# Exponentials on VectorE as four shifted piecewise linear terms, added by the value matmuls, with two PSUM banks for them and projections in 32-column pieces

## The chip, the cores and the metric

One core of one Trainium2 chip runs the program. The metric is the device time in microseconds (us) of one execution, as the median over the runs of a kernel. ACT is ScalarE, DVE is VectorE, PE is TensorE, POOL is GpSimd. The profile of a kernel is one more execution, taken with the hardware profiler; "the records" are that execution's instruction records, and times in them are counted from the first record.

## The reference

Four blocks follow each other: multi-query attention (A), linear attention (B), A, B, each with a layer norm ahead and a residual around it. S = 2048 tokens, D = 512, H = 32 heads of 16.

```python
def _A_ref(x, wq, wk, wv, wo):              # one K and V head for 32 query heads
    q = (x @ wq).reshape(B, S, H, Dh).transpose(0, 2, 1, 3)
    k, v = x @ wk, x @ wv
    p = softmax(einsum("bhqd,bkd->bhqk", q, k) * Dh ** -0.5)
    return merge(einsum("bhqk,bkd->bhqd", p, v)) @ wo
def _B_ref(x, wqkv, wo):
    phi = lambda t: where(t > 0, t + 1, exp(t)) + 1e-6
    pq, pk = phi(q), phi(k)
    kv, z = einsum("bhsd,bhse->bhde", pk, v), einsum("bhsd->bhd", pk)
    return merge(einsum("bhqd,bhde->bhqe", pq, kv) / (einsum("bhqd,bhd->bhq", pq, z) + 1e-6)) @ wo
x = x + _A_ref(_layernorm(x), ...);  x = x + _B_ref(_layernorm(x), ...)     # twice
```

Block A needs 2 x 32 x 2048 x 2048 exponentials, which is 2 x 2048 = 4096 tiles of 128 x 512.

## The kernel before

A scheduler, written in Python and run while the program is built, simulates the engines with planned durations and fixes the order of the instructions on each engine. On the chip each engine follows its fixed list and waits on semaphores. A lower `prio` goes first.

```python
# a score set: 32-row matmuls into 2 or 3 PSUM banks, one exponential on ScalarE, then value matmuls from PTA
o = add(PE, ..., prio=0.0, name="sA", pk=("S", ...))
oe = add(AC, tac(m * 512), lambda e: e.activation(PTA[:, hp.idx, 0:m * 512], bank(3 * s, m * 512), ACTF.Exp, scale=SCALE), ...)
...
# some tiles go to VectorE: scores in bank 6, six operations per pair of tiles
o = add(DV, tdv(512), lambda e: e.tensor_scalar(out=xT[...], in0=bank(6), scalar1=SCALE * LOG2E * 65536.0, scalar2=127.0 * 65536.0, ...))
... # dpass: xu, xsq, xw, xl, xc (fp16 polynomial), xo (scalar_tensor_tensor into PTD as uint16, read as bf16)
...
# a "unit" of 64 tiles fills the one value accumulator (bank 7); norm() then hands it on
oe = add((DV, AC), ..., lambda e: copy(Eo[:, he.idx, :], bank(7)), acq=[he], rel=[h7], prio=0.0, name="evA")      # 2 Eo buffers
o = add(PE, 0.48, tr, ..., acq=[ht, hos] if par == 0 else [ht], rel=[he], prio=1.2, name="trA")                   # one bank, one of 2 Osb
...
def epi_tr(L, qb, g, hos, fine):
    pr = 4.0
    o = add(PE, 0.22, tr, ..., acq=[h], uses=[hos], rel=[hos], prio=pr, name="otr")                               # one bank; gives Osb back
...
def phi(h, o, dst, keys, prio, tiled=False):          # keeps the bank of the projection until its last step
    o1 = add(AC, tac(512), lambda e: e.activation(e_buf[:, he.idx, :], bank(h.idx), ACTF.Exp), ..., name="phe")
    o2 = add(DV, tdv(512, 0.52), lambda e: e.tensor_scalar(out=e_buf[...], in0=e_buf[...], scalar1=1.0, scalar2=1e-6, op0=ALU.min, op1=ALU.add), ..., name="phm")
    add(DV, tdv(512), lambda e: e.scalar_tensor_tensor(out=dst, in0=bank(h.idx), scalar=0.0, in1=e_buf[...], op0=ALU.max, op1=ALU.add), rel=[h, he], ...)
...
# b_prep, pr = 3.5: the query projections of block B
o = proj(h, [(wqkv_sb[...], xnT[...]) for ft in range(FT)], 512, ..., pr + 0.2, name="pq")
...
# Banks.take for such single banks: 6, or else 5 while it is lent
elif f[6]: got = 6
elif f[5] and self.share(): got = 5
```

The softmax here doesn't subtract the row's maximum and nothing guards it: scores larger than these inputs give would overflow.

## Time and profile before

| | before |
|---|---|
| median of the first 3 runs | 1764.62 us (1764.61 to 1767.42) |
| PE, DVE, ACT, POOL busy | 92, 91, 97, 2 % |
| chain that ended last | ACT 89 %, DVE 5 %, PE 5 % |
| exponential tiles on VectorE | 512 of 4096 |
| time at half TensorE clock | 3.4 us, in the tail |

The lines themselves stand in the prediction. In a line of groups come the source line, engine and operation, the tiles written and read, their shapes, the number of instructions, the busy time, the mean of one in ns, and then the idle time of the engine just before them with what ended it. ACT is on 89 % of the chain and almost always busy, so the time is ACT's work in the attention stretches plus a rest.

For all kernels below I split the records of the profiled run in the same way, so that the parts sum to the span: the exponentials of the attention at their unhindered spacing from start to start (1.330 us after one 1536 wide, 0.904 us after one 1024 wide, 0.478 us after one 512 wide), ACT's other work between the first and last exponential of a layer, ACT's time lost between them (apart for full and half TensorE clock), and the rest: ramp, layer change and tail. Before: 1592.5 + 49 + 21.8 + 0 + 99.7 = 1763 us.

### The profile page before, as it was taken

The page shows a single profiled execution, that of the slowest core. Times are in us where ns is not written, and L with a number is a line of the kernel's source. Part 1 is how long each engine was busy: PE and PEld are TensorE (multiplying, and loading weights), DVE is VectorE, ACT ScalarE, POOL GpSimd, SP SyncE. Part 2 cuts the span into 40 slices and gives each one's busy share as a digit, 9 for nine tenths or more (in the row PEclk, how much of TensorE's full clock was granted, in tenths as well). Part 3 has the DMA queues.
Part 4 walks back from the last instruction along what each step waited for, and adds up shares of the span by engine and source line. Part 5 has one row for each costly group of instructions (what it writes and reads, how often), then busy time and mean ns, then how long its engine had stood idle before and what let it go on. Part 6 is the DMA issues. An engine that isn't in the chain of part 4 may idle for free.

```text
span 1762.9 us, 27663 instructions
## 1 busy us (share of the span) xinstructions
PE 1621.9 (92%) x11447; PEld 511.0 (29%) x11533; DVE 1601.6 (91%) x2902; ACT 1714.9 (97%) x1553; POOL 28.0 (2%) x46
## 2 busy tenths in 40 slices
PE   7999999999998899999799999999989999999998
PEld 4222222222232223223342222222223222232224
DVE  7999988999889998899589998899999999989985
ACT  7999999999999999999699999999999999999995
POOL 0000000000000000000000000000000000000000
PEclk9999999999999999999999999999999999999999
DMA  3000000000000000000000000000000000000001
GB/s 121 1 1 1 1 1 1 1 1 1 1 1 1 1 1 1 1 1 1 1 1 1 1 1 1 1 1 1 1 1 1 1 1 1 1 1 1 1 1 48
DMA packets 7725, 9.14 MB, mean 5 GB/s; under 512 B 1456, under 2 KB 7088, under 8 KB 7600
## 3 DMA queue, kind: packets, MB, share of 16 engines
q1 hardware_dynamic: 7600, 7.37, 1.3%
q8 instruction: 90, 1.47, 0.3%
q14 instruction: 35, 0.29, 0.1%
HBM read 5.28 MB, written 2.10 MB: 4 GB/s over the span
## 4 chain that ended last, share of the span: by engine, by line
ACT 89%; DVE 5%; PE 5%; DMA 0%; issue 0%; SPq 0%
ACT PTA L809 86%; ACT e_buf L991 2%; PE ps_all L522 1%; PE ps_all L1112 1%; PE ps_all L661 1%; DVE stats L487 1%; PE ps_all L698 1%; DVE PTD L885 1%; DVE xn_buf L498 0%; DVE Kr L537 0%; DVE xT L863 0%; DMA x_sb<-in_A_x_dram 0%; DVE xnT L511 0%; PE ps_all L1110 0%; DVE pqT L1106 0%
## 5 line engine op out<-in xcount | busy, mean ns | idle before, releaser
L809 ACT ACTIVATE PTA<-ps_all 128x1536 bf16<-128x1536 f32 (+1 forms) x1307 | 1630.7, 1520 | 2.3 <-PE ps_all L661 1.4
L661 PE MATMUL ps_all<-QT,Kr 32*128 32x512 bf16 x4226 | 652.5, 384 | 84.3 <-ACT PTA L809 66.4
L698 PE MATMUL ps_all<-PTA,Vaug 128*32 128x512 bf16 x3584 | 548.7, 389 | 15.7 <-ACT PTA L809 11.0
L863 DVE TENSOR_SCALAR xT<-ps_all 128x512 int32<-128x512 f32 x512 | 349.7, 683 | 28.4 <-PE ps_all L661 25.6
L661 PEld LDWEIGHTS ps_all<-QT,Kr 32*128 32x128 bf16 x4226 | 159.9, 91 | 578.1 <-ACT PTA L809 404.1
L885 DVE SCALAR_TENSOR_TENSOR PTD<-xT,xs 128x1024 uint16<-128x1024 int32 x256 | 310.4, 1214 | 0.6
L947 PE MATMUL ps_all<-maskx,zer 128*32 128x512 bf16 x911 | 296.2, 381 | 0.3 <-DVE Eo L710 0.3
L698 PEld LDWEIGHTS ps_all<-PTA,Vaug 128*32 128x32 bf16 x3584 | 134.6, 93 | 359.9 <-issue 253.2
L880 DVE TENSOR_SCALAR xu<-xT 128x1024 f16<-128x1024 uint16 x256 | 174.6, 682 | 1.2
L884 DVE TENSOR_TENSOR xs<-xs,xu 128x1024 f16<-128x1024 f16 x256 | 174.0, 681 | 1.2
L881 DVE TENSOR_TENSOR xs<-xu 128x1024 f16<-128x1024 f16 x256 | 174.1, 680 | 1.0
L698 PE MATMUL ps_all<-PTD,Vaug 128*32 128x512 bf16 x512 | 137.0, 387 | 3.5 <-DVE PTD L885 1.8
L882 DVE TENSOR_SCALAR xs<-xs 128x1024 f16<-128x1024 f16 x256 | 106.3, 415 | 0.8
L883 DVE TENSOR_SCALAR xu<-xu 128x1024 f16<-128x1024 f16 x256 | 106.5, 416 | 0.0
L947 PEld LDWEIGHTS ps_all<-maskx,zer 128*32 128x32 bf16 x911 | 80.1, 95 | 72.4 <-issue 41.5
L522 PE MATMUL ps_all<-wqkv_sb,xnT 128*128 128x512 bf16 x230 | 67.6, 390 | 4.8 <-issue 3.3
L992 DVE TENSOR_SCALAR e_buf<-e_buf 128x512 f32<-128x512 f32 x64 | 27.0, 421 | 33.7 <-ACT e_buf L991 33.6
L991 ACT ACTIVATE e_buf<-ps_all 128x512 f32<-128x512 f32 x64 | 44.9, 712 | 6.3 <-PE ps_all L522 4.3
L495 POOL TENSOR_TENSOR rstd<-veps,mhalf 128x1 f32<-128x1 f32 x30 | 24.5, 818 | 1657.0 <-DVE veps L493 1657.0
L487 DVE BATCH_NORM_STATS2 stats<-x_sb 128x6 f32<-128x512 bf16 x64 | 43.2, 682 | 3.5 <-DMA x_sb<-in_A_x_dram 2.8
L698 PEld LDWEIGHTS ps_all<-PTD,Vaug 128*32 128x32 bf16 x512 | 30.7, 93 | 54.3 <-DVE PTD L885 23.8
L719 PE MATMUL ps_all<-identf,Eo 128*128 128x128 f32 x256 | 42.0, 286 | 2.5 <-ACT Eo L710 1.4
(89 smaller groups left out, 842.3 us busy)
## 6 DMA issues: line engine op xcount, KB each, us to landing
out_dram<-x_sb SPq DMA_DIRECT2D x16, 128.0 KB, 1.7
x_sb<-in_A_x_dram SPq DMA_DIRECT2D x3, 512.0 KB, 6.8
wqkv_sb<-in_B_wqkv_dram SPq DMA_DIRECT2D x1, 1536.0 KB, 11.3
x_sb<-in_A_x_dram SPq DMA_DIRECT2D x2, 256.0 KB, 3.5
wq_sb<-in_A_wq_dram SPq DMA_DIRECT2D x1, 512.0 KB, 4.7
wo_sb<-in_A_wo_dram SPq DMA_DIRECT2D x1, 512.0 KB, 7.9
wo_sb<-in_B_wo_dram SPq DMA_DIRECT2D x1, 512.0 KB, 11.1
wk_sb<-in_A_wk_dram SPq DMA_DIRECT2D x1, 16.0 KB, 2.5
```

What stands on the lines that cost most here:

```text
L522: i = e.matmul(bank(h.idx, n), lhsT=l, rhs=r, start=(c + k == 0), stop=(c + k == len(mms) - 1))
L661: x = e.matmul(bank(b0 + k), lhsT=Kr[r, m, kt * P:(kt + 1) * P], rhs=QT[r, self.units[u][0] % 2, gs, q0:q0 + n], start=True, stop=True)
L698: return e.matmul(ps[32 * c:32 * c + 32, 7 * 512:8 * 512], lhsT=Vaug[:, kt, :], rhs=src, start=opened[0], stop=opened[1], skip_group_check ...
L809: oe = add(AC, tac(m * 512), lambda e: e.activation(PTA[:, hp.idx, 0:m * 512], bank(3 * s, m * 512), ACTF.Exp, scale=SCALE), deps=[o] + pr ...
L863: o = add(DV, tdv(512), lambda e: e.tensor_scalar(out=xT[:, hx.idx, i * 512:(i + 1) * 512], in0=bank(6), scalar1=SCALE * LOG2E * 65536.0, ...
L880: o = add(DV, tdv(w, 0.52), lambda e: e.tensor_scalar(out=u_, in0=lo, scalar1=1.0 / 65536, scalar2=-0.5, op0=ALU.mult, op1=ALU.add), deps= ...
L881: o1 = add(DV, tdv(w, 0.52), lambda e: e.tensor_tensor(out=s_, in0=u_, in1=u_, op=ALU.mult), deps=[o] + c["prev"], name="xsq", **kw)
L882: o2 = add(DV, tdv(w, 0.26), lambda e: e.tensor_scalar(out=s_, in0=s_, scalar1=XK, scalar2=-XW, op0=ALU.mult, op1=ALU.add), deps=[o1], nam ...
L883: o3 = add(DV, tdv(w, 0.26), lambda e: e.tensor_scalar(out=u_, in0=u_, scalar1=1.0, scalar2=XL, op0=ALU.mult, op1=ALU.add), deps=[o1], nam ...
L884: o4 = add(DV, tdv(w, 0.52), lambda e: e.tensor_tensor(out=s_, in0=s_, in1=u_, op=ALU.mult), deps=[o2, o3], name="xc", **kw)
L885: o5 = add(DV, tdv(w), lambda e: e.scalar_tensor_tensor(out=PTD[:, hp.idx, 0:w].bitcast(U16), in0=xT[:, k, 0:w], scalar=2.0 ** -9, in1=s_, ...
L947: f = lambda e: e.matmul(ps[32 * c:32 * c + 32, 7 * 512:8 * 512], lhsT=zer[:, 0:32], rhs=maskx[:].bitcast(BF16)[:, 0:512], start=not owned ...
```

## The change

It lets VectorE compute far more exponentials with less work each. It adds a bias to the scaled score and writes it as uint16, whose bits read as bf16 are a piecewise linear 2^x. Three copies with 32, 64 and 96 added shift the breaks. The value matmuls add the four terms, with weights folded into four scaled copies of V. VectorE gets two PSUM banks, ScalarE fixed sets of three and two. Projections are cut into four matmuls of 32 columns, so they run in the tiling mode of the value matmuls.

```diff
-            if len(c["pos"]) == 2:
+            if len(c["p1"]) == 4:
...
-            o = add(DV, tdv(w, 0.52), ... name="xu");  o1 ... "xsq";  o2 ... "xw";  o3 ... "xl";  o4 ... "xc"
-            o5 = add(DV, tdv(w), lambda e: e.scalar_tensor_tensor(out=PTD[:, hp.idx, 0:w].bitcast(U16), ...), name="xo")
+            for r in range(NTERM):
+                dep = c["p1"]
+                if r:
+                    dep = [add(DV, tdv(512 * m, 0.26), lambda e, r=r: e.tensor_scalar(out=PTD[:, hp.idx, r, 0:512 * m],
+                               in0=PTD[:, hp.idx, 0, 0:512 * m], scalar1=float(SHIFT[r]), scalar2=None, op0=ALU.add), ..., prio=3.0, name="xo")]
+                for i, p in enumerate(c["pos"]):
+                    pv = self.add_pv(p, PTD[:, hp.idx, r, i * 512:(i + 1) * 512].bitcast(BF16), hp, dep[0 if r else i], r, 1)
...
-    NPA, NPD, NDX = 5, 6, 3
+    NPA, NPD = 5, 3
...
+    DB = (5, 6)
...
-                w = 3
-                if s == 1 and SHARE and (not banks.free[5] or (not banks.free[6] and self.waiting())):
-                    w = 2
+                w = 3 - s
...
+    def mm(e, out, lhsT, rhs, start, stop):
+        for c in range(4):
+            i = e.matmul(out[32 * c:32 * c + 32], lhsT=lhsT[:, 32 * c:32 * c + 32], rhs=rhs, start=start, stop=stop, skip_group_check=True)
+        return i
...
+    sc.gate = lambda: ctl.layer is not None and not ctl.ramp and not ctl.tail
-    banks.sets_for_misc = lambda: (1, 0) if (...) else ((1,) if ctl.ramp else ())
+    def for_misc():
+        if ctl.tail or (ctl.ramp and not (ctl.layer is not None and ctl.ok(0))):
+            return (6, 5, 4, 3, 2, 1, 0)
+        return (6, 5, 4, 3) if ctl.ramp else (6,)
...
-        o2 = add(DV, tdv(512, 0.52), lambda e: e.tensor_scalar(out=e_buf[:, he.idx, :], ..., op0=ALU.min, op1=ALU.add),
+        o2 = add(PO, 0.65, lambda e: e.tensor_scalar(out=e_buf[:, he.idx, :], ..., op0=ALU.min, op1=ALU.add),
```

`sc.gate` switches on a new rule of the scheduler: TensorE work of another tiling mode is held back for up to 2 us until there is enough of it. The last two hunks: projections and transposes lose the second bank that they could borrow, and the clamp of the linear attention's feature map moves to GpSimd. Smaller hunks are left out here, among them other priorities (VectorE's score matmuls 1.5 to 0.01, the attention's later query projections 5.0 to 3.3), a look-ahead of 16 tiles for 26, and rings of eight buffers for keys and values of the linear attention.

## The prediction

> **What bounds the kernel now.** I read the page's busy shares first, then the chain that ended last, then the costliest groups.
>
> ```profile
> PE 1621.9 (92%) x11447; PEld 511.0 (29%) x11533; DVE 1601.6 (91%) x2902; ACT 1714.9 (97%) x1553; POOL 28.0 (2%) x46
> ACT 89%; DVE 5%; PE 5%; DMA 0%; issue 0%; SPq 0%
> ...
> L947 PE MATMUL ps_all<-maskx,zer 128*32 128x512 bf16 x911 | 296.2, 381 | 0.3 <-DVE Eo L710 0.3
> ```
>
> Three engines look full, but only ScalarE (ACT) is on the chain. It does most of the softmax exponentials (line 809). PE's 92% contains 911 matmuls on zeros (line 947), which the kernel's scheduler puts in only where PE would be idle. The two long attention stretches (32 to 845 us and 911 to 1720 us, cut where the chain breaks into short pieces) give, in the table of windows:
>
> ```profile
> core 0: us, PE busy (x) PEld busy (x) DVE busy (x) ACT busy (x) POOL busy (x), PEclk, DMA share, GB/s
> 32.00:845.00 813.00, 754.42 (x5250) 224.07 (x5286) 745.79 (x1318) 812.51 (x675) 11.92 (x15) 1.00 0.00 1
> 911.00:1720.00 809.00, 752.48 (x5204) 224.53 (x5235) 754.42 (x1331) 808.18 (x676) 12.60 (x15) 1.00 0.00 1
> ```
>
> ACT is busy 1620.7 of 1622 us, DVE 1500.2 (92.5%). The other 141 us (ramp, change of layer, tail) hold few exponentials. So the time is, to first order, ACT's exponentials plus a constant. By shape:
>
> ```profile
> L809 ACT ACTIVATE PTA<-ps_all 128x1536 bf16<-128x1536 f32 x970 | 1373.3, 1651 | 2.3 <-PE ps_all L661 1.4
> L809 ACT ACTIVATE PTA<-ps_all 128x1024 bf16<-128x1024 f32 x337 | 384.3, 1140 | 0.0
> ```
>
> The means are durations that overlap; what counts is the distance from one start to the next. In the trace's records its median is 1.330 us after a 1536-wide one and 0.904 us after a 1024-wide one. That makes 970 x 1.330 + 337 x 0.904 = 1595 us.
>
> **A wait that the busy share hides.** An exponential's record ends about 0.3 us after the next one may start, so a stall shorter than that leaves ACT "busy". After 1024-wide exponentials with a 1536-wide one next, the distance has mean 0.958 and ninth decile 1.127, against 0.904 unhindered: 0.054 us lost each time. After 1536-wide ones it is only 0.006 us. The timeline shows why:
>
> ```profile
> 1474.25 1.65 ACT L809 ACTIVATE PTA<-ps_all 128x1536 bf16<-128x1536 f32 x1
> ...
> 1475.96 0.40 PE L698 MATMUL ps_all<-PTA,Vaug 128*32 128x512 bf16 x3
> 1476.29 0.98 PE L661 MATMUL ps_all<-QT,Kr 32*128 32x512 bf16 x6
> ...
> 1476.73 1.45 ACT L809 ACTIVATE PTA<-ps_all 128x1536 bf16<-128x1536 f32 x1
> ```
>
> The wide exponential gives its three banks back at 1475.90. PE has a value pass first (1475.96), then the scores (1476.29); the next wide exponential starts at 1476.73, 1.14 us after the 1024-wide one before it (1475.59 in the records). Undisturbed, the loop is 0.29 (banks free after the narrow one's start) + 0.065 (scores start) + 0.56 (scores start to exponential start) = 0.915 us: no slack at all in the narrow one's 0.904.
>
> **The Trainium skill.** "VectorE: DVE Perf Modes", section "The perf-mode tier table", gives a single-source copy or tensor_scalar on 16-bit data in SBUF the 4x rate, and a PSUM operand at most 2x. Its section "What auto-detection actually checks" asks for element size and stride, not for float. The trace agrees: fp16 128x1024 on lines 882 and 883 took 415 ns, the fp32 PSUM source on line 863 683 ns for 512. No contiguous uint16 at 4x is in this trace, so that is inferred. "TensorEngine Tiling (Array Packing)", section "Key Properties", says that a change of tiling mode drains TensorE; the records agree: from the last scores to the first value matmul 0.314 us, against 0.216 between passes in one mode, so 0.10 us per change. "SBUF — State Buffer", section "Who interferes with whom", says that GpSimd and a 2-port VectorE mode block each other; GpSimd works for 28 us here, so the trace doesn't test it.
>
> **The change part by part**, with instruction counts from the two instruction orders.
>
> ACT. VectorE takes 997 score tiles of 4096 instead of 512. ACT keeps 632 exponentials 1536 wide, 601 1024 wide, one of 512: 632 x 1.330 + 601 x 0.904 + 0.5 = 1384 us instead of 1595, so **211 us less**. ACT's other work stays. The sets are now fixed, three banks and two, because two banks go to VectorE. Hence almost every wide exponential follows a narrow one: 601 such spots instead of 337.
>
> DVE. Before, the exponential cost by start-to-start 512 x 0.60 + 256 x (3 x 0.60 + 2 x 0.335 + 1.135) = 1230 us, 2.4 us a tile. After: 997 evictions x 0.60 = 598 us, and 750 shift adds on 2048 uint16. At 4x these take 415 ns + (1024 / 4) cycles[...] = 0.68 us, 0.60 us to the next: 450 us. The sum is 1048 us, 1.05 us a tile: less work than before for twice the tiles. 64 small operations (27 us by duration) move to GpSimd. Of the 1500 us in the two stretches about 1290 us remain.
>
> PE. Value matmuls rise from 4096 to 7087 (3099 + 4 x 997). Projections become four 32-column matmuls each, which run side by side, as the value matmuls in the trace do (starts 4 ns apart), and need no change of mode beside value matmuls. I counted passes (512 columns in each tile used, in program order) and changes of mode. Before: 4429 passes and 2943 changes without the zeros, x 0.216 and x 0.10 = 1251 us. After: 5285 and 2779 = 1420 us. So PE gets **170 us more real work while the span should shrink by 200**; the zero matmuls fall from 995 to 101, both shapes together. Weight loads could add some 20 to 40 us (an estimate from 25 ns per matmul on line 551 with 16 columns, if narrow tiles keep to that spacing), mostly in the ramps.
>
> Sum. Without any stall: 1763 - 211 = 1552 us, less the roughly 20 us of small stalls now in the exponentials (289 x 0.054 + 0.006 for the rest) = about 1532 us. Then stalls: 601 x 0.054 = 32 us if the narrow spots stay as they are. But in these stretches PE is fuller: over one wide and one narrow exponential (2.234 us) it has about 2.1 us of work (the same count, taken along the program, gives some 67 us for every 210 score matmuls, and such a pair goes with 6.6 of them: 5 of its own and 5 x 997 / 3099 = 1.6 for VectorE), where before a quarter was filler or free. Value runs grow to two or three passes, so the scores start late more often. I take 0.095 us a spot (57 us; a judgement, not derived). With a few us for GpSimd in the chain of the linear layers, the result is **1590 us**.
>
> **The rivals.**
>
> 1. ACT stays bound and never waits: 1535 us. For it: the scheduler places scores ahead of values, and before the change ACT hardly paused. At 1535, DVE would be 1290 / 1394 = 92.5% full in the stretches, as now, so the split fits this end. Against: the loop with no slack at 601 spots.
> 2. PE becomes the bound. Its 1420 us plus weight loads are a floor of 1440 to 1460 us, but PE runs strictly in order with two ACT buffers. If each narrow spot lost a whole value pass and a change of mode (0.2 us), it would be 1532 + 120 = about 1655 us. For it: 2.1 of 2.234 us. Against: part of that waits for nothing, and the two-bank set has 0.4 us of slack.
> 3. VectorE becomes the bound, because the uint16 shifts miss the 4x mode. At 2x each takes 1.13 us start to start: 750 x 0.53 = 400 us more, about 1690 us in the stretches alone, 1830 in all, slower than now. Against: line 880 already reads uint16 (stride two) and takes 682 ns for 1024, the 2-port rate, so uint16 is no obstacle by itself.
> 4. GpSimd and VectorE block each other around the 64 moved operations: up to about 0.5 us each, 30 us in all, less where VectorE has slack.
>
> **Range and chances.** The low end, 1540, is rival 1 with almost no stalls; the high end, 1650, is rival 2 near its full cost. I give rivals 1 and 2 a tenth each beyond those ends; rival 3 gets 0.02. Faster by over 2% means below 1729, which all but rival 3 and an unexpected cost meet: 0.95, within 2% 0.03, slower 0.02.
>
> **What would show it right or wrong.** The shift adds (line 911) should take about 0.68 us each, the evictions (line 894) 0.68; 1.2 us in line 911 is rival 3. The start-to-start distance after a 1536-wide exponential should stay near 1.33; after a 1024-wide one it should have a mean near 1.00. Near 0.91 is rival 1, 1.1 or more is rival 2. PE should show almost no zero matmuls, DVE about 90% in the stretches. ACT should stay near 97% busy on the page, as short stalls hide in it, and still lead the chain, with PE's share above 5%. The clock should stay near 1.0. The number fails if ramp, layer change and tail (141 us) grow by tens of us through narrow matmuls or GpSimd, or if PE's passes cost more than 0.216 us with narrow tiles.

## The result, and the profile after

The changed kernel took **1688.97 us** (1684.60 to 1696.03, 4 runs) against 1766.02 us (1764.61 to 1768.15, 4 runs). The ratio is 0.9564, 95 % interval 0.954 to 0.9589: 4.4 % faster. All ratios here are the mean time of one kernel's fast runs over that of the other's fast runs of the same rounds, so not quite the ratio of the medians. The direction was right; 1590 us was not, nor was the range of 1540 to 1650 us.

The page of the kernel after: busy shares, granted clock in 40 slices (in tenths), and the shares of the chain that ended last.

```profile
PE 1602.4 (95%) x18333; PEld 531.1 (31%) x18333; DVE 1415.1 (84%) x2525; ACT 1530.4 (90%) x1496; POOL 170.5 (10%) x157
...
PEclk9999999999999799999999988899999999999999
...
PE 45%; ACT 34%; DVE 13%; POOL 6%; issue 2%; DMA 0%; SPq 0%; POOLq 0%; ACTq 0%
```

ACT fell from 97 to 90 %, the chain now runs mostly through PE, GpSimd has got a share of it, and the clock dips in four slices. The table of windows for the two attention stretches (window, length, then busy time and instructions of PE, PEld, DVE, ACT and POOL, then clock, DMA share and GB/s):

```profile
30.00:790.00 760.00, 725.61 (x7472) 227.95 (x7470) 653.65 (x1138) 712.20 (x645) 63.64 (x49) 0.98 0.01 1
855.00:1630.00 775.00, 744.91 (x7515) 230.59 (x7513) 660.12 (x1154) 721.89 (x659) 60.21 (x52) 0.97 0.01 1
```

ACT is idle for 101 of 1535 us, where before it was idle for 1.3 of 1622. The groups, ACT's exponentials by shape first:

```profile
L844 ACT ACTIVATE PTA<-ps_all 128x1536 bf16<-128x1536 f32 x632 | 933.1, 1476 | 72.6 <-PE ps_all L688 68.9
L844 ACT ACTIVATE PTA<-ps_all 128x1024 bf16<-128x1024 f32 x601 | 632.6, 1053 | 17.1 <-PE ps_all L688 16.3
```

Then VectorE's two new groups, and GpSimd's clamp:

```profile
L894 DVE TENSOR_SCALAR PTD<-ps_all 128x512 uint16<-128x512 f32 x997 | 676.3, 684 | 153.4 <-PE ps_all L688 149.0
L911 DVE TENSOR_SCALAR PTD<-PTD 128x2048 uint16<-128x2048 uint16 (+1 forms) x750 | 499.3, 684 | 5.0
L1023 POOL TENSOR_SCALAR e_buf<-e_buf 128x512 f32<-128x512 f32 x64 | 126.6, 1978 | 701.7 <-ACT e_buf L1022 686.0
```

The counts are as forecast, the shift adds took 684 ns, and ACT now waits for scores (line 688). One line is a surprise: the clamp (line 1023) takes 1978 ns on GpSimd. The split of the records says where the missing time is: 1383 (exponentials) + 45.8 (other) + 100.6 lost at full clock + 43.8 lost around half clock + 121.1 (ramp, layer change, tail) = 1694 us, the span of the profiled run.

The worst single place is between 572 and 588 us. In the timeline of the kernel after (start, duration, engine, line, operation, tiles; in brackets the idle time of the engine before it and what ended it):

```profile
574.84 0.60 ACT L1022 ACTIVATE e_buf<-ps_all 128x512 f32<-128x512 f32 x1 [4.73 <-PE ps_all L459]
575.52 1.92 POOL L1023 TENSOR_SCALAR e_buf<-e_buf 128x512 f32<-128x512 f32 x1 [3.41 <-ACT e_buf L1022]
577.47 0.69 DVE L1026 SCALAR_TENSOR_TENSOR pqT<-ps_all,e_buf 128x512 bf16<-128x512 f32 x1 [3.43 <-POOL e_buf L1023]
578.22 1.90 PE L459 MATMUL ps_all<-xnT,wqkv_sb 128*32 128x512 bf16 x16 [3.43 <-DVE pqT L1026]
580.16 0.60 ACT L1022 ACTIVATE e_buf<-ps_all 128x512 f32<-128x512 f32 x1 [4.73 <-PE ps_all L459]
580.85 1.92 POOL L1023 TENSOR_SCALAR e_buf<-e_buf 128x512 f32<-128x512 f32 x1 [3.41 <-ACT e_buf L1022]
582.80 0.69 DVE L1026 SCALAR_TENSOR_TENSOR pqT<-ps_all,e_buf 128x512 bf16<-128x512 f32 x1 [4.63 <-POOL e_buf L1023]
583.54 0.60 PE L998 MATMUL ps_all<-ident,Osb 128*128 128x128 bf16 x4 [3.43 <-DVE pqT L1026]
...
584.67 1.12 PE L746 MATMUL ps_all<-identf,Eo 128*128 128x128 f32 x4 [0.52 <-DVE OT L1004]
585.82 0.69 DVE L737 COPY Eo<-ps_all 128x512 f32<-128x512 f32 x1 [1.21 <-PE ps_all L746]
...
587.54 0.61 PE L688 MATMUL ps_all<-QT,Kr 32*128 32x512 bf16 x3
...
588.20 1.45 ACT L844 ACTIVATE PTA<-ps_all 128x1536 bf16<-128x1536 f32 x1 [7.44 <-PE ps_all L688]
```

Every engine stands still in turn. The query projections (line 459) go one after the other, 5.3 us each: projection, exponential, clamp, last step, and only then the next projection, as if there were one bank. Then come, in this order, the transposes out of Osb (998), the transposes out of Eo (746), the eviction of the accumulator into Eo (737), and only then a score set (688). The time from one eviction of the accumulator to the next is 44.2 us here, against a median of 23.6. TensorE runs at half clock from 567.3 to 591.2 us: the sixteen matmuls of a projection take 1.90 us, where the run e1 below shows the same sixteen in 1.05 us at full clock.

### The profile page after: what moved, and what is told of

Same layout as the page of the kernel before. It is cut to its first block, busy times and chain, and to the rows that moved or that the text cites.

```text
span 1694.3 us, 40968 instructions
## 1 busy us (share of the span) xinstructions
PE 1602.4 (95%) x18333; PEld 531.1 (31%) x18333; DVE 1415.1 (84%) x2525; ACT 1530.4 (90%) x1496; POOL 170.5 (10%) x157
## 4 chain that ended last, share of the span: by engine, by line
PE 45%; ACT 34%; DVE 13%; POOL 6%; issue 2%; DMA 0%; SPq 0%; POOLq 0%; ACTq 0%
ACT PTA L844 32%; PE ps_all L688 18%; PE ps_all L725 17%; PE ps_all L459 6%; POOL e_buf L1023 6%; DVE PTD L894 4%; DVE PTD L911 3%; PE ps_all L746 2%; ACT e_buf L1022 1%; DVE pk_tok L1026 1%; DVE pqT L1026 1%; DVE Eo L737 1%; DVE stats L512 1%; PE ps_all L971 1%; PE ps_all L530 1%
## 5 line engine op out<-in xcount | busy, mean ns | idle before, releaser
L844 ACT ACTIVATE PTA<-ps_all 128x1536 bf16<-128x1536 f32 (+1 forms) x1234 | 1430.7, 1269 | 89.7 <-PE ps_all L688 85.3
L894 DVE TENSOR_SCALAR PTD<-ps_all 128x512 uint16<-128x512 f32 x997 | 676.3, 684 | 153.4 <-PE ps_all L688 149.0
L688 PE MATMUL ps_all<-QT,Kr 32*128 32x512 bf16 x4201 | 721.5, 388 | 21.7 <-DVE PTD L894 10.3
L725 PE MATMUL ps_all<-PTD,Vaug 128*32 128x512 bf16 x3988 | 586.4, 392 | 9.7 <-DVE Eo L737 7.6
L911 DVE TENSOR_SCALAR PTD<-PTD 128x2048 uint16<-128x2048 uint16 (+1 forms) x750 | 499.3, 684 | 5.0
L725 PEld LDWEIGHTS ps_all<-PTD,Vaug 128*32 128x32 bf16 x3988 | 143.5, 95 | 198.8 <-issue 128.2
L1023 POOL TENSOR_SCALAR e_buf<-e_buf 128x512 f32<-128x512 f32 x64 | 126.6, 1978 | 701.7 <-ACT e_buf L1022 686.0
L459 PE MATMUL ps_all<-wqkv_sb,xnT 128*32 128x512 bf16 x1024 | 81.6, 386 | 8.5 <-DVE pk_tok L1026 7.1
L459 PE MATMUL ps_all<-xnT,wq_sb 128*32 128x128 bf16 (+1 forms) x896 | 44.8, 301 | 3.5 <-issue 3.4
L737 DVE COPY Eo<-ps_all 128x512 f32<-128x512 f32 x63 | 42.9, 681 | 1.9 <-PE ps_all L746 1.2
L746 PEld LDWEIGHTS ps_all<-identf,Eo 128*128 128x128 f32 x256 | 28.6, 148 | 32.2 <-DVE pk_tok L1026 12.7
```

Of the source, the lines that this page charges most:

```text
L459: i = e.matmul(out[32 * c:32 * c + 32], lhsT=lhsT[:, 32 * c:32 * c + 32], rhs=rhs, start=start, stop=stop, skip_group_check=True)
L688: x = e.matmul(bank(b0 + k), lhsT=Kr[r, m, kt * P:(kt + 1) * P], rhs=QT[r, self.units[u][0] % 2, gs, q0:q0 + n], start=True, stop=True)
L725: return e.matmul(ps[32 * c:32 * c + 32, 7 * 512:8 * 512], lhsT=Vaug[:, kt, r, :], rhs=src, start=opened[0], stop=opened[1], skip_group_ch ...
L737: return (e.copy if oe.eng == AC else e.tensor_copy)(Eo[:, he.idx, :], bank(7))
L746: i = e.transpose(bank(ht.idx, P, qs * P), Eo[:, he.idx, qs * P:(qs + 1) * P], identf[:])
L894: o = add(DV, tdv(512), lambda e: e.tensor_scalar(out=PTD[:, hp.idx, 0, i * 512:(i + 1) * 512], in0=bank(db), scalar1=SCALE * LOG2E * 128. ...
```

## The experiments

Each was timed in three rounds against the kernel before; all results were correct. The first table has them all; the parts are from the split of the profiled run. "Lost" is ACT's time between the exponentials in which it does nothing else, a stall; "half" is the part of it from 1 us before to 3 us after a stretch at half clock. How a stall at the edge of such a stretch is counted moves up to 13 us (in e1) between the two columns, not their sum.

| run | median us | ratio to before | exponentials | lost, full clock | lost, half | ramp, change, tail | half clock, us |
|---|---|---|---|---|---|---|---|
| before | 1766.0 | 1 | 1592.5 | 21.8 | 0 | 99.7 | 3 |
| after | 1689.0 | 0.9564 | 1383.0 | 100.6 | 43.8 | 121.1 | 92 |
| e1_dve_clamp | 1664.1 | 0.9434 | 1383.0 | 80.7 | 45.9 | 108.8 | 72 |
| e2_plan_gpsimd | 1689.1 | 0.9579 | 1382.6 | 76.4 | 54.3 | 132.6 | 85 |
| e3_more_filler | 1744.7 | 0.9887 | 1384.3 | 119.8 | 59.9 | 128.7 | 85 |
| e4_full_width | 1749.6 | 0.9903 | 1382.9 | 94.6 | 109.9 | 126.7 | 174 |
| e5_otr | 1679.4 | 0.9520 | 1382.9 | 107.1 | 31.7 | 118.9 | 72 |
| e6_otr_npa6 | 1653.2 | 0.9370 | 1392.5 | 72.1 | 32.2 | 118.7 | 68 |
| e7_clamp_otr | 1629.4 | 0.9231 | 1383.0 | 78.1 | 4.7 | 116.1 | 10 |
| e8_clamp_otr_npa6 | 1608.6 | 0.9116 | 1392.5 | 53.2 | 3.6 | 116.1 | 7 |
| e9_gps_planned | 1631.9 | 0.9241 | 1388.5 | 63.2 | 0 | 133.2 | 14 |
| e10_one_bank | 1621.5 | 0.9186 | 1403.2 | 55.7 | 4.6 | 118.3 | 14 |
| e11_clamp_pq_npa6 | 1599.9 | 0.9069 | 1392.0 | 51.3 | 0.3 | 110.9 | 7 |
| e12_clamp_otr_pta9 | 1614.2 | 0.9149 | 1420.6 | 35.7 | 0.2 | 106.5 | 7 |
| e13_lend_bank5 | 1628.8 | 0.9217 | 1383.5 | 82.6 | 4.4 | 114.8 | 14 |
| e14_no_gate | 1626.3 | 0.9205 | 1382.0 | 83.6 | 0 | 115.4 | 0 |

ACT's other work is 40 to 49 us in all and left out. Of e4's 20 runs ten were slow; its median and ratio are of the ten fast ones. Its profile fell in the slow state (half clock 174 us), so its parts don't compare with the others.

### First call: GpSimd, the clock, and the projections

**e1_dve_clamp**: the clamp back on VectorE.

```diff
-        o2 = add(PO, 0.65, lambda e: e.tensor_scalar(out=e_buf[:, he.idx, :], ...
+        o2 = add(DV, 0.345, lambda e: e.tensor_scalar(out=e_buf[:, he.idx, :], ...
```

> The clamp inside phi (64 operations) back from GpSimd to VectorE, planned at 0.345 us; the split of score tiles is the same (997 on VectorE). Theory G (the 1.92 us GpSimd operation stalls the in-order engines, and the clock drops follow from those stalls): single ACT stalls over 0.5 us fall from 67 us to under 15, half-clock time from 92 us to under 30, time about 1600 us (1580 to 1625). Rival P (TensorE is simply too full; the GpSimd waits are hidden): time 1660 us or more, half-clock time unchanged near 90 us.

It gained 25 us (1664.1). The clamp itself is 4.6 times as fast there; the list of that line's durations (minimum, median, maximum in ns, then first and last start), for the kernel after:

```profile
L1023 POOL TENSOR_SCALAR e_buf<-e_buf x64: 1919/1922/2422, 116.6 to 1684.1; 128x512 f32<-128x512 f32 x64
```

and e1:

```profile
L1023 DVE TENSOR_SCALAR e_buf<-e_buf x64: 411/417/429, 116.1 to 1634.0; 128x512 f32<-128x512 f32 x64
```

12 of the 25 us lie in ramp, change and tail, the others in the layers. But 72 us of half clock remained, and 74 of the 99 us that were missing. The expectation of theory G, 1580 to 1625 us, failed. So GpSimd was a real cost and not the main one.

**e2_plan_gpsimd**: the clamp stays on GpSimd, and the scheduler plans 1.95 us for it.

```diff
-        o2 = add(PO, 0.65, ...
+        o2 = add(PO, 1.95, ...
```

> The clamp stays on GpSimd; only the scheduler's figure for it goes from 0.65 to 1.95 us, so the static order is made for what it takes. Theory G in its first form (the order is made for 0.65 us, and every engine waits in order for the surprise): 1610 to 1635 us. Second form (the 1.9 us itself holds the one free PSUM bank and the chain, whatever the order): 1665 us or more. Rival P: 1680 to 1695 us, as the change.

1689.1 us, no change. At this point that seemed to say that the plan doesn't matter. The trace of e2 has two intervals of 49 and 48 us between evictions, at 531 and 1415 us, where the kernel after has one, so the gain could be hidden by another loss; e9 repeats the test without them.

**e3_more_filler**: more matmuls on zeros, against the clock drops.

```diff
-    AWIN, ATGT, ATGT2 = 1.7, 0.5, 0.6
+    AWIN, ATGT, ATGT2 = 1.7, 0.7, 0.8
```

> The change with the threshold for zero matmuls raised from 0.5 to 0.7 (305 instead of 101 of them). Rival C (the clock drops are a cause of their own: too little TensorE activity was planned): half-clock time from 92 us to under 20, time about 1645 us. Theory G (stalls come first, and filler behind a waiting in-order TensorE cannot run): half-clock time stays over 50 us, time within 15 us of 1689.

1744.7 us: 56 us slower, which neither theory expected, with 85 us of half clock for 92. So more filler did not keep the clock up. What it cost by itself isn't shown: 204 more zero matmuls at 0.216 us are about 44 us of TensorE time (an estimate), but this order also has two intervals of 53 and 46 us between evictions, at 1408 and 597 us.

**e4_full_width**: each projection as one 128-column matmul again.

```diff
-    ALL4 = ("P", (0, 1, 2, 3))
+    ALL4 = ("F", ())
-        for c in range(4):
-            i = e.matmul(out[32 * c:32 * c + 32], lhsT=lhsT[:, 32 * c:32 * c + 32], ...)
-        return i
+        return e.matmul(out, lhsT=lhsT, rhs=rhs, start=start, stop=stop, skip_group_check=True)
```

> The projections as one 128-column matmul each, as before the change, rest as changed: 13642 instead of 18333 matmuls, 5436 instead of 5377 passes, 2938 instead of 2802 changes of mode. If narrow tiles cost nothing extra and TensorE is not the bound: within 10 us of 1689. If TensorE's passes bound it: 59 x 0.216 + 136 x 0.1 = 26 us more, about 1715. If narrow matmuls are what made it slower than forecast (weight loads, issue): 1650 or less.

1749.6 us in the fast runs: taken back, this part costs about 60 us, outside all three expectations. Whether that is the width of the matmuls isn't shown. At full width the projections are also in the mode of the transposes, so the new rule holds them back too, and the order that comes out has two intervals of 54 and 70 us between evictions, at 544 and 1417 us. In its profile (a slow run) 109.9 us are lost around half clock for 43.8 with the change, which is as much as the whole difference. No run takes the narrow projections back with the bank order mended. Ramp, change and tail took 126.7 us at full width and 121.1 with the change, so nothing there speaks for the fear that narrow matmuls fill them.

### Second call: who holds bank 6, and the buffers at a hand-over

I followed the static order through the stretch shown above. When a unit's 64 tiles are summed, its accumulator (bank 7) must be copied into one of two Eo buffers (a hand-over, below). Both hold older units whose transposes (trA, priority 1.2) have not run. These need one of two Osb buffers, and both are waiting for their own transposes (otr, priority 4.0). Those need a single bank. There is one, bank 6, and four query projections (priority 3.7) take it first, each for as long as its feature map lasts. No value matmul of the next unit may start meanwhile, so all PTA buffers fill and no score set may be issued. A priority of 1.2 waits for one of 3.7, through two pools of two buffers.

**e5_otr**: one number.

```diff
 def epi_tr(L, qb, g, hos, fine):
-        pr = 4.0
+        pr = 3.3
```

> One number changed in the kernel after: the transposes of finished heads get a better priority (3.3 for 4.0), ahead of the second block's query projections (3.7). Theory B, a chain on PSUM bank 6: the eviction of a full value accumulator waits for one of two Eo buffers, these for transposes that wait for one of two Osb buffers, these for transposes that wait for bank 6, and bank 6 goes to four query projections first, of some 4 us each; no score set can be issued meanwhile. B expects the stretch at 560 to 591 us (unit interval of 44 us instead of 23) to be gone: some 18 us less of stalls, and the 24 us at half clock that follow it gone too (12 us): 1655 to 1665 us, half clock below 70 us in the profile. Theory C, the clock falls for the mean load whatever the order is: half clock stays at 80 to 95 us somewhere else, 1668 to 1675 us. If the bubble has another cause, nothing moves: 1685 us and the 44 us interval stays.

The long interval at 542 us went, and with it the drop at 567 us. But the time was 1679.4 us, 10 us less and not the 24 to 34 expected: two other drops, at 996 and 1054 us, stayed (27 and 14 us, at 1004 and 1062 us in the kernel after). The order explains one of the places and not these two. The clock row of e5's page:

```profile
PEclk9999999999999999999999988899999999999999
```

The clock row of e5 above (40 slices again) has lost the first dip of the kernel after and kept the second.

**e6_otr_npa6**: also a sixth PTA buffer, with one e_buf less for room.

```diff
-    NXN, NE = 3, 4
+    NXN, NE = 3, 3
-    NPA, NPD = 5, 3
+    NPA, NPD = 6, 3
```

> As e5_otr, and with a sixth PTA buffer (one e_buf less, for room). Theory H, the ScalarE stalls of 0.5 to 2 us after each hand-over of the single accumulator bank come from full PTA buffers: another buffer carries ScalarE over the hand-over. H expects 15 to 30 us below e5_otr (big warm stalls near hand-overs halved, 1630 to 1645 us), less about 8 us given back because about 20 tiles go from VectorE to ScalarE. The rival, that TensorE is short of time there whatever the buffers, expects the same time as e5_otr or up to 8 us more.

1653.2 us, 26 us below e5, in spite of 20 fewer tiles on VectorE. Stalls of over 0.5 us at full clock fell from 72 to 33 us, those within 3 us of a hand-over from 40 to 16. So the buffers were the limit at most hand-overs, not TensorE's time.

**e7_clamp_otr**: the clamp on VectorE and the better priority.

> As e5_otr, with the clamp on VectorE as in e1_dve_clamp (1664 us), which has two such stretches (563 to 583 and 1381 to 1403 us) and 72 us at half clock, 65 of them right at these two. B expects both stretches and the half clock at them gone: 38 us plus about 30 us, 1595 to 1615 us, half clock below 20 us. C expects the 38 us alone: 1624 to 1632 us, half clock 60 us or more. Nothing moves if the cause is another.

1629.4 us, 35 us below e1. Both long intervals (42 and 43 us in e1) are gone, and half clock fell from 72 to 10 us. I had expected 1595 to 1615 because I added the stalls in the stretches and the half clock there as two sums. They are one: the stretches lie in half clock, and that column fell by 41 us in all (45.9 to 4.7). In the tenths of e7's clock row no dip is left:

```profile
PEclk9999999999999999999999999999999999999999
```

The rival, a clock that falls for the mean load, wanted 60 us or more of half clock. It is out: PE is busier here (97 %) than in e1 (96 %).

**e8_clamp_otr_npa6**: all three.

> Clamp on VectorE, better priority of the transposes and the sixth PTA buffer together. B with H expects 1580 to 1600 us, which would beat both kernels and come near the 1590 us that was predicted; without H the time of e7_clamp_otr or up to 8 us more.

1608.6 us, 9 us above the range that was expected. Stalls over 0.5 us fell from 42 us (e7) to 20, again at the hand-overs (31 to 11).

### Third call: plan or duration, one bank, the other way round, more buffers

**e9_gps_planned**: e6 with 1.95 us planned for GpSimd's clamp.

> As e6_otr_npa6 (clamp on GpSimd, 1653 us), but the scheduler plans 1.95 us for it instead of 0.65. Theory P: what GpSimd cost (45 us between e6 and e8) is mostly a wrong plan, so that TensorE's fixed order waits for operations that are not done; P expects 1615 to 1630 us and half clock below 25 us. Theory D: the 1.92 us itself, 64 times on the path that holds the only free PSUM bank, is what costs, planned or not; D expects 1645 to 1660 us and half clock 50 us or more.

1631.9 us against 1653.2 in e6 and 1608.6 in e8. With the bank order mended, the plan is worth 21 us and 54 us of half clock; the duration itself costs the other 23 us, of which 17 lie in ramp, change and tail (133.2 against 116.1). So both theories hold about half. That e2 showed nothing fits its two long intervals, which could hide a gain of this size.

**e10_one_bank**: e8, with one bank for VectorE's exponentials.

```diff
-    DB = (5, 6)
+    DB = (5,)
```

> As e8_clamp_otr_npa6 (1608.6 us), but VectorE's exponentials get one PSUM bank (5) instead of two (5 and 6); bank 6 is then for projections and transposes alone. 951 tiles instead of 976 go to VectorE, so ScalarE's exponentials take 1405 us instead of 1394. If the second bank matters beyond that share, stalls grow: 1630 us or more. If it does not, and bank 6 being shared costs as much as it brings: 1610 to 1622 us.

1621.5 us, 13 us more, of which 11 are ScalarE's larger share (951 tiles on VectorE for 976). The second bank is worth that and little else.

**e11_clamp_pq_npa6**: as e8, but the transposes keep 4.0 and the query projections go behind them.

```diff
-                pq_tile(t, pr + 0.2)
+                pq_tile(t, pr + 0.8)
...
-                             ["wqkv"] + [...], pr + 0.2, name="pq")
+                             ["wqkv"] + [...], pr + 0.8, name="pq")
```

> As e8_clamp_otr_npa6, but the order between transposes and query projections is put right from the other side: the transposes keep 4.0 and the query projections go from 3.7 to 4.3. Theory B (the order between these two alone is what matters) expects no long interval between hand-overs, and 1600 to 1615 us; if the better time of e8 came from something else that the priority 3.3 moved (3.3 is also ahead of the other projections at 3.5), the stretches without scores come back: 1630 us or more.

**1599.9 us** (1597.03 to 1605.49), ratio 0.9069: the best of all, 9.3 % faster than before and 5.3 % by the medians below the change as it was. Its page:

```profile
PE 1553.7 (97%) x18294; PEld 523.8 (33%) x18294; DVE 1409.2 (88%) x2561; ACT 1528.3 (96%) x1498; POOL 43.8 (3%) x94
...
L844 ACT ACTIVATE PTA<-ps_all 128x1024 bf16<-128x1024 f32 (+1 forms) x1244 | 1431.2, 1279 | 20.1 <-PE ps_all L688 16.6
```

ACT is 96 % busy again, and its idle time ahead of exponentials fell from 89.7 us (after, both forms: 72.6 + 17.1) to 20.1. That the order of these two groups can be mended from either side supports the chain.

**e12_clamp_otr_pta9**: e7 with nine PTA and two PTD buffers.

```diff
-    NPA, NPD = 5, 3
+    NPA, NPD = 9, 2
```

> As e7_clamp_otr (1629.4 us), with nine PTA buffers and two PTD buffers instead of five and three. Theory H: the big stalls at hand-overs (e7: 42 us, e8 with six PTA: 20 us) go to below 8 us; but only 912 tiles go to VectorE, so the exponentials on ScalarE take 1422 us instead of 1383. Net: 1629 + 39 - 36 = 1632 us, 1620 to 1640. If the stalls don't depend on PTA buffers beyond six, 1640 us or more.

1614.2 us, better than I expected. Big stalls came to 9 us, as the theory of the buffers says, and small ones fell as well (36 to 27). The 38 us of exponentials that went back to ScalarE ate most of it.

### Fourth call: which part of the change made the chain

The two priorities, 4.0 and 3.7, were there before the change, whose longest interval inside a layer was 30 us.

**e13_lend_bank5**: e1, and a free bank 5 may be borrowed as before.

```diff
-        return (6, 5, 4, 3) if ctl.ramp else (6,)
+        return (6, 5, 4, 3) if ctl.ramp else (6, 5)
```

> As e1_dve_clamp (1664.1 us, two stretches without scores, 72 us at half clock), but projections and transposes may take bank 5 as well when it is free, as the kernel before allowed; priorities unchanged (transposes 4.0, query projections 3.7). If the chain exists because the change left projections and transposes one single bank, both stretches go and the time comes to that of e7_clamp_otr: 1620 to 1640 us, half clock below 20 us. If a second bank only lets more projections in ahead of the transposes, it stays at 1655 to 1675 us.

**e14_no_gate**: e1, without the new rule that keeps PE work of another mode back.

```diff
-    sc.gate = lambda: ctl.layer is not None and not ctl.ramp and not ctl.tail
+    sc.gate = lambda: False
```

> As e1_dve_clamp, but without the rule that the change added to the scheduler, which holds TensorE work of another tiling mode back (up to 2 us) unless there is enough of it. If this rule is what makes the transposes (full-width mode) lose bank 6 to the 32-column query projections, the stretches go: 1620 to 1640 us if grouping the modes saved little, more if it saved mode changes. If the priorities alone are to blame, the stretches stay: 1655 to 1675 us.

1628.8 and 1626.3 us, the same as e7 within 3 us, with the longest intervals at 33 us and below 28 us and half clock at 14 and 0 us. Either one takes the chain apart. So it needs both: one bank left for everything, and a rule that keeps the full-width transposes waiting while 32-column projections, now in the mode of the value matmuls, may go at once. The rule saved nothing for this: the instruction order of e14 has 2822 changes of mode, that of e1 2838.

Every edit changes the whole order, so one may ask whether the long intervals come and go by luck. The five orders without any of these mends (after, e1 to e4) all have one of 42 us or more inside a layer, and the ten with one of them (e5 to e14) have none above 36 us.

### What stays open

The two drops at 1004 and 1062 us in the kernel after went when the clamp was faster (e7) or planned right (e9), but with six buffers and the wrong plan (e6) they came at other places. I take them for the result of TensorE waiting behind GpSimd, but no run isolates them. What the narrow projections are worth by themselves is open (e4), and so is why e11 is 9 us faster than e8. Ramp, layer change and tail are 11 us longer in e11 than before (110.9 for 99.7); I did not look for the cause.

## Why the prediction was wrong, point by point

1. **ACT's exponentials, 1384 us: right.** The split has 1383, with medians from start to start of 1.331 and 0.905 us.
2. **VectorE: right.** The shift adds took 684 ns (0.68 forecast), the evictions 684 ns; rival 3 is out, and contiguous uint16 does get the 4x rate that was inferred for it. (The 256 cycles in that forecast are 0.27 us by the kernel before: lines 880 and 882, 1024 elements at half and at full rate, differ by 682 - 415 ns.) VectorE was 86 % busy in the stretches, not about 90 %, as it waited with the others.
3. **TensorE's work: right.** 101 zero matmuls were left, the records without them change mode 2778 times (2779 forecast), and a pass of a narrow projection took 0.216 us from start to start (median, 512 columns), so the last sign, dearer narrow passes, did not come. Rival 2, TensorE as the bound through a value pass at each narrow spot, is not what happened: e7, e8 and e11 do nearly the same matmuls in 60 to 89 us less.
4. **Narrow spots, 57 us, "a judgement": right in size, by luck.** After 1024-wide exponentials the mean distance at full clock was 1.009 us in the kernel after: 568 x (1.009 - 0.904) = 60 us. But about 31 of these are 30 stalls of over 0.5 us, 19 of the 31 within 3 us of a hand-over. The short waits for late scores that the prediction describes cost 0.052 us a spot (539 spots, 28 us), as before the change (0.054), so its own 32 us for "if the narrow spots stay as they are" was right, and the raise to 0.095 because value runs grow was not. In e11 the short ones cost 0.051.
5. **"Sum. Without any stall: ... Then stalls: 601 x 0.054 ...": this step failed.** It let ScalarE stall only at the narrow spots, and left ramp, layer change and tail (141 us by its windows, 99.7 by the split here) as they were. The records of the kernel after have, beside the 60 us of point 4, about 40 us at full clock elsewhere (100.6 - 60), among them 35 us after 1536-wide exponentials (546 x 0.034 and ten gaps of 1.63 us more), 43.8 us around half clock and 21 us more in ramp, change and tail. That is 105 us, against 104 us between 1590 and the profiled run: the whole miss. The causes that the runs show are the clamp on GpSimd (25 us, e1), the chain on bank 6 (35 us, e1 to e7) and the PTA buffers at the hand-over of the one accumulator (21 us, e7 to e8): some 80 us. e8 is 19 us above 1590, e11 10 us. Rival 1, no waiting at all, is out.
6. **"With a few us for GpSimd": wrong.** I took 27 us of VectorE time, moved, for the cost of the move, and did not ask how long GpSimd takes. It takes 1.92 us for 0.42, planned as 0.65, on a path that holds the only free bank: 25 us (e1), 45 us once the chain is gone (e6 to e8).
7. **Rival 4, GpSimd and VectorE blocking each other: it exists and is small.** 28 shift adds that overlapped the clamp took 0.758 us in the mean (1.108 at most) for 0.682 otherwise, about 2 us in all. The 21 clamps beside them took 2.08 us for 1.93 of the others (2.42 at most), about 3 us. Evictions from PSUM beside it took 0.685 us for 0.684. "Up to about 0.5 us each" holds for the longest only. The section that the prediction cites ("SBUF — State Buffer", "Who interferes with whom", in the Trainium skill) lets whoever issues first keep the shared ports for the whole instruction, and here that isn't so: of the seven shift adds that began in a clamp's first 0.45 us, six ended 0.76 to 0.77 us before the clamp did, and six of the seven that began later inside one were not held at all (0.68 to 0.70 us). So the clamp seems to hold the ports for about the first 0.5 of its 1.92 us (an estimate: 1.92 - 0.77 - 0.68).
8. **"The clock should stay near 1.0": wrong** for the kernel after (0.973 in the profile), right for e7 (0.997) and e11 (0.998). I took the clock for a matter of load. In these runs it went with the stalls: where they went, it stayed up.
9. **"ACT should stay near 97% busy ... and still lead the chain": wrong** (90 %, and 34 % of the chain for PE's 45 %) for the same reason: short stalls hide in the busy share, these did not. "With PE's share above 5%" was right, and far too low.

With the causes of 5, 6 and 8 gone, e11 stands at 1600 us, and its exponentials (1392.0) and its stalls (51.6) are close to the sums of 1384 and 57 behind 1590, the second in part by luck (point 4). What the change saves was read correctly; what it costs through the shared resources that it narrowed was not.

## What to carry to other kernels

When a change takes a bank or a buffer from a pool, follow every waiter of that pool through to its end: here a one-bank pool and a scheduling rule let a low priority hold up the eviction that everything waited for, and one number undid it. When an operation moves to another engine, measure its duration there and put it into the plan, as a fixed order pays for the error twice. Test suspects together as well as alone: the corrected plan showed nothing while the long intervals were there (e2), and 21 us without them (e9).

## What the Trainium skill lacked or had wrong

- "GPSIMD Engine Reference", section "4.1 Engine selection", says that operations with one input run roughly at line rate. Here a tensor_scalar with two operations on 128 x 512 fp32 took 1.92 us on GpSimd and 0.42 us on VectorE (an eviction of 128 x 512 fp32 from PSUM, also two operations, 0.68 us). The VectorE operation that needs it starts 1.95 us after it (575.52 to 577.47), so this is no artefact of the record.
- "TensorE: Matmul & The Clock Gate", Part 1, names idle windows of about 3.4 us as what brings half clock; its section "A second HAM failure mode: psum-queue depth-cycling" adds that frequent short idle times between groups of matmuls do it too, without saying how much is too much. In these runs no idle window is needed: in the 3.40 us before the drop at 1587.8 us of the kernel after PE was busy for 2.92 us, and the longest idle time was 0.21 us. If a 32-row matmul is counted as a quarter (a weighting that no run tests by itself), all 71 drops in the sixteen profiles came after 3.4 us with a mean of 0.05 to 0.64, where the median of the kernel after is 0.83. It isn't sufficient: of the kernel after's 465 windows at full clock about 50 were below 0.70, and 9 of them led to a drop. That drops last multiples of 3.4 us and share one phase in a run agrees with the page.
- "ScalarE: Activation LUTs", section "Rules for kernel authors", calls ScalarE the only option for exp. In the kernel after VectorE makes 997 of 4096 tiles of exponentials, at 1.05 us a tile (997 x 0.60 + 750 x 0.60 us from start to start) beside ScalarE's 0.44 to 0.45 us a tile.
